# Sliding-window attention and token mixing on one core: permuted channels, weights staged in the mixing buffers, two batches of natural q and k, held stores and a new order

## The chip, the cores and the metric

The kernel runs on one core of one Trainium2 chip. The metric is the device time of one execution in microseconds (us). Three runs of the kernel before gave 143.59, 143.82 and 145.14 us, a median of 143.82 us.

The core has a matrix engine (TensorE, PE in the profile, with its weight loads as PEld), a vector engine (DVE), an activation engine (ACT), a general engine (POOL) and a queue engine (SP). Each runs its own instructions strictly in order. In this kernel POOL does almost nothing but issue the loads that change 32-bit inputs into 16-bit tiles, SP issues weight loads and stores, and ACT and DVE share the work of moving results out of PSUM, the memory that PE writes.

## The reference

Attention with a causal window of 128 tokens and a bias that falls with distance, for 8 batches of 8 heads, 576 tokens and 64 values a head; then a token-mixing layer over the 512 joined channels:

```python
scores = scale * np.matmul(q, k.transpose(0, 1, 3, 2))
mask = (rel >= 0) & (rel < window)
scores = np.where(mask, scores + bias[None], -1000000000.0)
attn = np.exp(scores - np.max(scores, axis=-1, keepdims=True))
attn = attn / (np.sum(attn, axis=-1, keepdims=True) + 1e-09)
x = np.matmul(attn, v)          # then heads joined: (8, 576, 512)
wq = x @ w_q
wk = x @ w_k                    # both 512 -> 64
W_tok = scale * np.einsum('bsd,btd->bst', wq, wk)
mixed = np.einsum('bst,btd->bsd', W_tok, x)
out = np.maximum(mixed, 0.0) @ w_out
```

## The kernel before, in words

**Attention.** The 576 tokens of a batch are four tiles of 128 and a tail of 64. POOL loads q, k and v with a cast to 16 bits, one DMA of 128 tokens x 8 heads x 64 values at a time (`Lq`, `Lk`, line 364; `Lv`, line 381; the q and k tails of two batches in `Lt`, line 371). In HBM such a tile is 1024 runs of 256 bytes. Three tiles of batch 0 are instead loaded in 32 bits by SP and ACT (`LF`, line 401) into buffers that later hold output. PE transposes q and k (`TF`, `TJ`, `TQ`, `TT`, line 235) and ACT or DVE copies them to `qkT` (`EF`, `EJ`, `ETQ`, `ETT`, lines 239 and 241). For each batch there are eight units of scores (`QK`, four key tiles times two groups of four heads): 64-row matmuls into a pair of PSUM banks, one exponential of 128 x 1024 on ACT (`EXP`, line 588) into one of the `pt` tiles, and one multiplication by the exponentiated bias and mask on DVE (`MUL`, line 595). `PV` multiplies with v, which carries a column of ones, so the sums come along. `RC` (line 649) takes reciprocals, and `X` (line 635, DVE) writes the normalised 128 x 512 tile of x in 16 bits: 32 full tiles and 8 tails of 64 rows.

**Mixing.** It is done once for each pair of batches: x is transposed (`XT`, `XTT`, copied by `EXT`, `EXTT`), then come the projections `WK`, `WQ`, `WT` with their copies `EWK`, `EWQ`, `EWT`; `G` is wk transposed times x, 64 x 512 for each batch, copied by `EG`; `MX` is the mixed tile in transposed form, to which `RM` and `RMT` (lines 771 and 773) apply the maximum with zero and write the 16-bit tile `rm`; `OUT` is four accumulating matmuls of 512 columns with `w_out`; `EO` copies the result to one of 12 32-bit output buffers (`osb`), and SP stores it (`DO`, lines 833 and 836).

**Weights.** `wz` is a memset on DVE that holds the weight loads back until DVE has come to it. `Lw` (line 441) loads `w_q` and `w_k`, in runs of 256 bytes, `Lwo` (line 449) `w_out` in four blocks of 128 rows of 2 KB. All go through SP into output buffers (`osb`). `CWQ` and `CW` copy them to 16-bit tiles, `CWQ` on ACT, `CW` on ACT and DVE. Every projection needs `CWQ`; every `OUT` needs the four `CW`.

**Order.** Nothing is scheduled automatically. A text lists every step with its engine and its PSUM bank, and each engine runs its steps in that order; waits come from data and from buffers being reused. For example `QK2.1.0:P3` is batch 2, key tile 1, head group 0, on PE, into bank pair 3; the letters A, D, G and S stand for ACT, DVE, POOL and SP. `WM` steps are matmuls on zeros whose result nobody reads. Every DMA also waits on its queue for the DMA eight places ahead of it on the same kind of queue (POOL's, or SP's and ACT's together) to land. Natural q and k tiles are kept for four batches, so a load of batch b waits for the transposes of batch b - 4; `pt` has five slots of two tiles, so an exponential waits for the `PV` steps five key tiles earlier.

Of the kernel before, what the change touches and what calls it, by code (L numbers as in the profile page):

```python
# [8 lines left out]
FP32 = mybir.dt.float32  # L9
# [5 lines left out]
P = 128  # L15
# [10 lines left out]
NNAT = 4  # L26
NV = 4
NPT = 5
# [5 lines left out]
OSB = 12  # L34
WIDE = ()

WARM = (13, 8, 2, 1, 2, 1, 4, 1, 9, 2, 6, 2, 9, 7, 1, 2, 2)

ORDER = """
warm:D LF0.0.1.1:A iota:G LF0.1.0.0:S WM.0:P01 ident:G LF0.0.1.0:A LF0.0.0.0:S wmc:D ones:D  # L40
LF0.0.0.1:S mask:G LF0.1.0.1:S Lk0.1:G bias:A Lq0.2:G idh:D TF0.1.0:P00 WM.1:P01 Lk0.2:G
EF0.1.0:D zeros:D Lk0.3:G TF0.0.0:P00 WM.2:P10 EF0.0.0:A TF0.0.1:P01 WM.3:P20 Lt0:G EF0.0.1:A
QK0.0.0:P1 TF0.1.1:P00 EXP0.0.0:A WM.4:P20 EF0.1.1:D TJ0.1.1:P01 QK0.0.1:P2 WM.5:P30 MUL0.0.0:D
Lq0.3:G EXP0.0.1:A TJ0.2.0:P00 WM.6:P30 EJ0.1.1:D Lk1.1:G EJ0.2.0:D TJ0.2.1:P10 biasl:D
QK0.1.0:P0 WM.7:P30 Lq1.1:G TJ0.3.1:P11 QK0.1.1:P2 WM.8:P31 Lq1.0:G EXP0.1.1:A MUL0.0.1:D
# [10 lines left out]
MUL1.2.1:D ETQ2.3:A PV1.1:P3 Lk2.0:G MUL1.3.1:D XT0.1:P21 RC1.0:D PV1.2:P1 RC1.1:D Lv1.4:G
pads:D EXT0.1:A wz:D X1.1:D Lwo.1:S Lv0.4:G Lw:S ETQ2.2:A X1.0:D PV1.3:P3 Lt1:G RC1.2:D Lwo.3:S
XT1.0:P00 RC1.3:D X1.2:D Lwo.0:S QK2.2.0:P2 Lwo.2:S EXT1.0:A X1.3:D TQ2.1:P01 Lq3.0:G ETQ2.1:D
XT1.1:P10 EXP2.2.0:A TQ2.0:P11 Lk3.0:G EXT1.1:A PV1.4:P0 ETQ2.0:D Lq3.1:G QK2.1.1:P3 RC1.4:D
QK2.0.0:P1 X1.4:D CWQ:A PV0.4:P2 Lk3.1:G EXP2.1.1:A WK0:P00 RC0.4:D X0.4:D Lq3.3:G EXP2.0.0:A  # L60
QK2.1.0:P3 EWK0:D QK2.0.1:P2 Lq3.2:G EXP2.1.0:A XTT0:P01 WQ0:P10 EXTT0:D Lv2.1:G EXP2.0.1:A
MUL2.1.0:D WT0:P11 Lk3.2:G MUL2.1.1:D TT2:P00 EWT0:A EWQ0:A CW.1:D G0:P01 ETT2:A ETT3:D CW.2:D
CW.3:A QK2.3.0:P1 EG0:D EXP2.3.0:A CW.0:D Lv2.3:G MX0.1:P0 MX0.0:P2 RM1.1:D MX0.3:P3 RM0.1:A
MX0.2:P1 Lv2.0:G RM1.3:A RM0.3:D TQ3.0:P00 RM1.0:A Lk3.3:G QK2.2.1:P3 ETQ3.0:D RM1.2:A TQ3.1:P01
EXP2.2.1:A RM0.2:D Lv2.2:G OUT1.0:P00 ETQ3.1:D RM0.0:A Lv3.0:G QK2.3.1:P1 MUL2.2.0:D QK3.0.0:P3
EXP2.3.1:A QK3.0.1:P2 MUL2.3.0:D Lk4.2:G OUT1.3:P01 MUL2.0.1:D EXP3.0.1:A OUT1.1:P10 Lk4.1:G
MUL2.3.1:D EXP3.0.0:A MUL2.2.1:D OUT0.1:P11 Lt2:G MUL2.0.0:D EO1.3:A TQ3.2:P20 EO1.0:A
MUL3.0.0:D PV2.1:P3 EO0.1:A ETQ3.2:D Lq4.2:G PV2.0:P0 DO1.0:S TQ3.3:P21 EO1.1:A RC2.1:D
OUT0.3:P11 X2.1:D Lv3.1:G ETQ3.3:A RC2.0:D PV2.3:P3 X2.0:D Lq4.1:G EO0.3:A QK3.1.0:P2 RC2.3:D
QK3.2.0:P0 X2.3:D EXP3.1.0:A Lv3.2:G PV2.2:P1 MUL3.0.1:D OUT1.2:P30 EXP3.2.0:A Lv3.3:G  # L70
MUL3.1.0:D XT2.0:P31 RC2.2:D Lv3.4:G EO1.2:A MUL3.2.0:D QK3.1.1:P2 QK3.3.0:P0 EXP3.1.1:A Lk4.3:G
X2.2:D OUT0.0:P30 EXT2.0:D Lq4.3:G EXP3.3.0:A QK3.3.1:P1 QK3.2.1:P2 EO0.0:D TT4:P31 Lq4.0:G
EXP3.2.1:A MUL3.1.1:D MX0.4:P0 OUT0.2:P30 MUL3.3.0:D RMT0:A Lk4.0:G PV3.0:P2 MUL3.2.1:D
EXP3.3.1:A TQ4.2:P00 Lv2.4:G ETT4:D TQ4.1:P01 ETT5:A RC3.0:D MUL3.3.1:D PV3.1:P1 Lq5.0:G EO0.2:A
OUT1.4:P31 X3.0:D ETQ4.2:A DO0.2:S Lq5.2:G RC3.1:D PV3.3:P2 DO0.0:S X3.1:D ETQ4.1:A DO0.1:S
XT2.1:P30 Lk5.0:G RC3.3:D DO0.3:S X3.3:D PV3.2:P1 EXT2.1:A Lk5.2:G QK4.1.1:P0 RC3.2:D PV3.4:P2
X3.2:D EXP4.1.1:A XT3.0:P30 Lq5.1:G RC3.4:D X3.4:D XT3.1:P10 TQ4.0:P11 Lk5.1:G EXT3.1:A EXT3.0:D
TQ4.3:P00 PV2.4:P2 Lq5.3:G ETQ4.0:D ETQ4.3:A WK2:P30 RC2.4:D Lk5.3:G X2.4:D QK4.0.1:P1 EWK2:A
MUL4.1.1:D QK4.2.0:P0 Lv4.0:G XTT2:P20 EXP4.0.1:A WQ2:P21 EXTT2:D Lv4.1:G EXP4.2.0:A WT2:P20
EWQ2:D QK4.3.1:P1 EWT2:A QK4.1.0:P0 MUL4.0.1:D EXP4.3.1:A G2:P30 Lv4.2:G EO1.4:D EXP4.1.0:A  # L80
DO1.4:S QK4.0.0:P2 EG2:D TQ5.2:P10 Lq6.2:G EXP4.0.0:A DO1.3:S MUL4.1.0:D MX2.0:P0 DO1.1:S
QK4.2.1:P3 RM2.0:D Lk6.2:G DO1.2:S EXP4.2.1:A MX2.2:P2 TQ5.0:P11 RM3.0:D Lv4.3:G RM3.2:A
ETQ5.2:D MX2.3:P3 MX2.1:P0 RM2.2:A Lq6.3:G RM2.1:D TQ5.1:P10 RM2.3:A TQ5.3:P20 RM3.1:D ETQ5.1:A
Lq6.1:G OUT2.1:P21 ETQ5.0:D RM3.3:A Lk6.1:G ETQ5.3:D QK4.3.0:P0 QK5.0.0:P1 EXP4.3.0:A QK5.0.1:P3
MUL4.0.0:D Lk6.0:G OUT2.0:P20 MUL4.2.0:D EXP5.0.1:A Lv5.1:G OUT3.1:P00 MUL4.2.1:D EO2.1:A
MUL5.0.1:D PV4.1:P3 EO2.0:A Lv4.4:G OUT2.3:P01 RC4.1:D EXP5.0.0:A MUL4.3.0:D PV4.2:P2 X4.1:D
EO2.3:A QK5.2.1:P1 RC4.2:D PV4.0:P3 X4.2:D EXP5.2.1:A OUT3.0:P01 Lv5.0:G RC4.0:D X4.0:D EO3.1:A
QK5.1.1:P2 QK5.1.0:P1 EO3.0:D EXP5.1.1:A QK5.2.0:P3 Lq6.0:G XT4.0:P00 MUL4.3.1:D OUT3.2:P01
EXP5.2.0:A EXT4.0:D Lk6.3:G MUL5.0.0:D QK5.3.0:P2 EO3.2:A Lv5.2:G PV4.3:P3 MUL5.2.1:D EXP5.1.0:A
TQ6.2:P00 Lk7.0:G RC4.3:D OUT3.3:P01 MUL5.1.1:D EXP5.3.0:A X4.3:D Lv5.3:G TQ6.1:P10 ETQ6.2:A  # L90
MUL5.2.0:D MX2.4:P2 QK5.3.1:P3 Lq7.0:G ETQ6.1:D OUT2.2:P11 EXP5.3.1:A MUL5.1.0:D Lv5.4:G
# [67 lines left out]
def kernel(  # L159
# [53 lines left out]
    def natv(b, j, n):  # L213
        return nat_s[(b // 2) % 2][j][n][:, b % 2]
# [95 lines left out]
    def mk_ones(o):  # L310
        for i in range(2):
            nc.vector.memset(vt_s[i][4][64:128], 0.0)
            for t in vt_s[i]:
                nc.vector.memset(t[:, :, :, D:D + 1], 1.0)
# [596 lines left out]
```

## Time and profile before

| What | Value |
|---|---|
| Median of three runs | 143.82 us |
| The profiled execution | 145.0 us |
| Its span, first to last instruction | 143.1 us |
| Outside the span | 1.9 us |
| Granted TensorE clock | 1.00 throughout |
| Busy: PE, DVE, ACT, POOL | 129.3, 117.5, 118.7, 95.3 us |
| HBM read, written | 29.62 MB, 9.44 MB |

Busy time by stage, from the windows of the profile, in us:

| Stage (us from the start) | length | PE | DVE | ACT | POOL |
|---|---|---|---|---|---|
| 0 to 36 | 36.0 | 30.59 | 27.60 | 27.73 | 35.16 |
| 36 to 48 | 12.0 | 8.52 | 7.83 | 8.95 | 8.94 |
| 48 to 124 | 76.0 | 75.41 | 73.10 | 74.01 | 51.15 |
| 124 to 143.1 | 19.1 | 14.75 | 9.00 | 7.99 | 0.00 |

Busy shares are averages over stages that have different limits. POOL's busy time is the issue of loads. A matmul's busy time includes its way through the array, so PE can look busier than it is. A wait is put down to whatever came last; a line number can be that of a helper that many steps share, so the operands tell which step is meant.

### The profile page before, as it was taken

How to read it: one execution, taken by the hardware profiler on the slowest of the kernel's cores; microseconds unless marked ns; L12 is line 12 of the kernel's file. 1: busy time of each engine (PE TensorE's matmuls, PEld its weight loads, DVE VectorE, ACT ScalarE, POOL GpSimd, SP SyncE). 2: the span in 40 equal slices, each digit the busy share in tenths (PEclk: the TensorE clock that was granted, in tenths of full speed). 3: DMA queues.
4: the chain of work that ended last, by engine and by line, in shares of the span. 5: the costliest groups of instructions: out<-in, count | busy, mean ns of one | idle time of the engine just before them, and what ended most of it. 6: DMA issues, size and time to landing. Idle time of an engine off the chain costs nothing.

```text
span 143.1 us, 4562 instructions
## 1 busy us (share of the span) xinstructions
PE 129.3 (90%) x1888; PEld 86.8 (61%) x1888; DVE 117.5 (82%) x253; ACT 118.7 (83%) x166; POOL 95.3 (67%) x118
## 2 busy tenths in 40 slices
PE   7979898589496999999998999999999999999980
PEld 4737776378263557678855466787665557863430
DVE  5478499988557999999879999999999999939720
ACT  4956967979398999999899999999999999867140
POOL 7999999999839999899949759998570000000000
PEclk9999999999999999999999999999999999999999
DMA  4999999999999999999999999999999941504494
GB/s 101 240 155 154 156 155 156 155 154 167 262 172 157 154 155 182 161 151 211 252 164 181 241 206 157 155 184 248 163 235 283 215 161 73 220 5 136 125 390 161
DMA packets 119333, 25.60 MB, mean 179 GB/s; under 512 B 114192, under 2 KB 114192, under 8 KB 119312
## 3 DMA queue, kind: packets, MB, share of 16 engines
q0 software_dynamic: 109264, 13.77, 151.9%
q1 hardware_dynamic: 8992, 11.28, 23.9%
q10 hardware_dynamic: 1056, 0.26, 0.8%
q8 instruction: 15, 0.25, 0.6%
q14 instruction: 6, 0.05, 0.1%
HBM read 29.62 MB, written 9.44 MB: 273 GB/s over the span
## 4 chain that ended last, share of the span: by engine, by line
PE 56%; POOL 15%; DMA 9%; DVE 7%; ACT 7%; issue 2%; SPq 0%; POOLq 0%; ACTq 0%
PE pair L232 46%; PE pair L235 11%; POOL nat L364 10%; DMA osb<-in_moe_w_k_dram 5%; DMA nat<-in_q_dram 5%; ACT pt L588 4%; POOL vt L381 3%; DVE rm L773 2%; DVE qkT L241 1%; POOL natt L371 1%; DVE osb L241 1%; DVE pt L595 1%; ACT wqT L239 1%; DVE x L635 1%; DVE wqT L241 0%
## 5 line engine op out<-in xcount | busy, mean ns | idle before, releaser
L588 ACT ACTIVATE pt<-pair 128x1024 f16<-128x1024 f32 x64 | 62.6, 1033 | 5.6 <-PE pair L232 5.1
L381 POOL DMA_DIRECT2D vt<-in_v_dram x40 | 34.7, 900 | 4.3 <-PE pair L232 2.1
L595 DVE TENSOR_TENSOR pt<-pt,bias 128x1024 f16<-128x1024 f16 x48 | 31.4, 680 | 2.9 <-ACT pt L588 2.8
L364 POOL DMA_DIRECT2D nat<-in_k_dram x31 | 28.8, 937 | 5.5 <-DMA natt<-in_k_dram 2.7
L232 PE MATMUL pair<-wout_sb,rm 128*128 128x512 f16 x128 | 31.1, 380 | 0.0
L364 POOL DMA_DIRECT2D nat<-in_q_dram x30 | 28.1, 947 | 0.7 <-PE pair L232 0.6
L232 PE MATMUL pair<-vt,pt 128*128 128x65 f16 x576 | 24.0, 193 | 1.1 <-DVE x L635 0.5
L232 PEld LDWEIGHTS <-pt 128*128 128x128 f16 x576 | 21.2, 97 | 6.3 <-issue 2.9
L232 PE MATMUL pair<-qkT 64*128 64x256 f16 (+2 forms) x320 | 21.6, 250 | 1.0 <-ACT pt L588 0.7
L635 DVE TENSOR_TENSOR x<-pair,inv 128x512 f16<-128x512 f32 x32 | 21.8, 687 | 0.8
L235 PE MATMUL pair<-identh,nat 128*128 128x128 f16 x244 | 18.6, 219 | 1.6 <-DMA nat<-in_k_dram 0.8
L239 ACT COPY osb<-pair 128x512 f32<-128x512 f32 x25 | 14.5, 609 | 5.0 <-PE pair L232 5.0
L232 PEld LDWEIGHTS <-rm 128*128 128x128 f16 x128 | 11.2, 98 | 11.7 <-issue 0.6
L235 PEld LDWEIGHTS <-nat 128*128 128x128 f16 x244 | 14.5, 97 | 5.5 <-DMA nat<-in_k_dram 1.9
L241 DVE COPY qkT<-pair 128x1024 f16<-128x1024 f16 (+1 forms) x26 | 15.2, 592 | 2.2 <-PE pair L235 1.1
L232 PEld LDWEIGHTS <-qkT 64*128 64x128 f16 x320 | 11.1, 94 | 8.5 <-issue 5.4
L239 ACT COPY qkT<-pair 128x1024 f16<-128x1024 f16 (+1 forms) x15 | 13.5, 916 | 0.9 <-PE pair L235 0.9
L232 PE MATMUL pair<-warm 128*128 128x256 f16 x72 | 12.0, 299 | 1.6 <-DVE warm L282 1.1
L239 ACT COPY xT<-pair 128x1024 f16<-128x1024 f16 x12 | 12.1, 1027 | 1.1 <-PE pair L235 0.8
L595 DVE TENSOR_TENSOR pt<-pt,biasl 128x1024 f16<-128x1024 f16 x16 | 10.8, 681 | 0.4 <-ACT pt L588 0.2
L771 ACT ACTIVATE rm<-pair 128x512 f16<-128x512 f32 x18 | 9.7, 618 | 0.6 <-PE pair L232 0.6
L235 PE MATMUL pair<-identh,x 128*128 128x128 f16 x128 | 9.6, 219 | 0.5 <-ACT pt L588 0.5
(69 smaller groups left out, 135.9 us busy)
## 6 DMA issues: line engine op xcount, KB each, us to landing
out_dram<-osb SPq DMA_DIRECT2D x32, 256.0 KB, 4.4
vt<-in_v_dram POOLq DMA_DIRECT2D x32, 128.0 KB, 6.8
nat<-in_k_dram POOLq DMA_DIRECT2D x31, 128.0 KB, 6.3
nat<-in_q_dram POOLq DMA_DIRECT2D x30, 128.0 KB, 6.5
osb<-in_moe_w_out_dram SPq DMA_DIRECT2D x4, 256.0 KB, 6.9
out_dram<-osb SPq DMA_DIRECT2D x8, 128.0 KB, 4.3
osb<-in_q_dram SPq DMA_DIRECT2D x4, 128.0 KB, 3.6
natt<-in_q_dram POOLq DMA_DIRECT2D x4, 128.0 KB, 6.1
```

The source lines that it names most:

```text
L232: hold(nc.tensor.matmul(*a, **k))
L235: hold(nc.tensor.transpose(*a))
L239: hold(nc.scalar.copy(out_ap, in_ap))
L241: hold(nc.vector.tensor_copy(out=out_ap, in_=in_ap))
L364: return lambda: nc.gpsimd.dma_start(out=natv(b, j, n), in_=(q, k)[j][b, :, P * n:P * n + P, :].transpose([1, 0, 2]))
L371: nc.gpsimd.dma_start(out=natt_s[pr % 2][:, j].rearrange("p e h d -> p (e h) d"), in_=(q, k)[j][2 * pr:2 * pr + 2, :, 512:576, :].rearrang ...
L381: return lambda: nc.gpsimd.dma_start(out=vtv(b, t)[:n, :, 0:D], in_=v[b, :, P * t:P * t + n, :].transpose([1, 0, 2]))
L588: nc.scalar.activation(out=pt[:, 0:1024], in_=two(s.bank).rearrange("p e c -> p (e c)"), func=AF.Exp, scale=SCALE)
L595: ENG2[o.eng].tensor_tensor(out=pt[:, 0:1024], in0=pt[:, 0:1024], in1=bt, op=ALU.mult)
L635: nc.vector.tensor_tensor(out=x[r].rearrange("p (g h d) -> p g h d", g=2, h=4), in0=sums(p)[r, :, :, 0:64], in1=box["inv"][r].unsqueeze(3) ...
L771: hold(nc.scalar.activation(out=out_ap, in_=in_ap, func=AF.Relu, scale=WSCALE))
L773: hold(nc.vector.tensor_scalar(out=out_ap, in0=in_ap, scalar1=0.0, scalar2=WSCALE, op0=ALU.max, op1=ALU.mult))
```

## The change

- **Channels of x.** `X` writes column `128*c + p` of its tile with channel `4*p + c`, so its four parts of 128 columns hold every fourth channel. The weights' rows are taken in the same way: `w_q` and `w_k` are each read as 128 runs of 1 KB, `w_out` in two loads of 128 runs of 4 KB.
- **Staging.** The weights lie, until they are cast, in the two `rm` buffers instead of the output buffers; the first `RM` steps wait for the casts. `wz` is two memsets. `CWQ` also turns the order of its columns.
- **Buffers.** Natural q and k for two batches instead of four, `pt` with eight slots instead of five, 15 output buffers instead of 12.
- **Held stores.** From batch 3 on, a step `GT b.g` on SP makes the next store wait for the first `QK` of that key tile; it issues nothing by itself.
- **Last output.** Tile 3 of batch 7 is made in two halves of 256 columns, each with its own copy and store.
- **Order.** A new text. `pads` moves to the start. 107 matmuls on zeros instead of 72. Between ACT and DVE some copies change places.
- Groups of batches become a table; all groups are still pairs, and the code for single batches is not used.

The core of the diff:

```diff
-NNAT = 4
+NNAT = 2
-NPT = 5
+NPT = 8
-OSB = 12
+OSB = 15
+GATES = 3
+GROUPS = ((0, 1), (2, 3), (4, 5), (6, 7))
+SPLIT = ((7, 3),)
...
-    nat_s = [[[cpool.tile([P, 2, H, D], F16, name=f"nat{i}{j}{n}") for n in range(4)]
-              for j in range(2)] for i in range(2)]
+    nat_s = [[[cpool.tile([P, H, D], F16, name=f"nat{i}{j}{n}") for n in range(4)]
+              for j in range(2)] for i in range(NNAT)]
...
+            wst = [t.rearrange("p d e t -> p (d e t)").bitcast(FP32) for t in rm_s]
+            def mk_wz(o):
+                for t in wst:
+                    nc.vector.memset(t[:, 0:1], 0.0)
...
-                    nc.sync.dma_start(out=dst[:, :, 64 * j:64 * j + 64],
-                                      in_=w.rearrange("(c p) j -> p c j", p=P))
+                    nc.sync.dma_start(out=wst[0][:, 256 * j:256 * j + 256],
+                                      in_=w.rearrange("(p c) j -> p (c j)", p=P))
...
-                      lambda o: cp(o.eng, wqk_sb.rearrange("p c j -> p (c j)"), wide32("qk")))
+                      lambda o: cp(o.eng, wqk_sb.rearrange("p c (m j) -> p m c j", m=2),
+                                   wst[0][:, 0:512].rearrange("p (m c j) -> p m c j", m=2, c=4)))
...
-                    out=wide32(c), in_=moe_w_out[P * c:P * c + P, :]))
+                    out=wst[1][:, 1024 * u:1024 * u + 1024],
+                    in_=moe_w_out.rearrange("(p c) n -> p (c n)", p=P)[:, 1024 * u:1024 * u + 1024]))
...
+        if u == 0 and b >= GATES:
+            add("GT", b, g, w, {"SP": (0.02, 0.02)}, [s], lambda o: gates.append(s))
...
-                out=x[r].rearrange("p (g h d) -> p g h d", g=2, h=4),
-                in0=sums(p)[r, :, :, 0:64],
-                in1=box["inv"][r].unsqueeze(3).broadcast_to([n, 2, 4, 64]),
+                out=x[r].rearrange("p (c g h t) -> p g h t c", c=4, g=2, h=4),
+                in0=sums(p)[r, :, :, 0:64].rearrange("p g h (t c) -> p g h t c", c=4),
+                in1=box["inv"][r].unsqueeze(3).unsqueeze(4).broadcast_to([n, 2, 4, 16, 4]),
                 op=ALU.mult)
...
+            old = [osd.get((x, st)) for x in prev for st in range(4)] if prev else [*wto, wts]
...
+    def gated(i):
+        while gates:
+            tc.add_manual_dep(
+                i.ins, gates.pop().insts[-1].name,
+                mybir.DependencyInfo(mybir.DependencyClass.Sync, mybir.DependencyReason.DATA),
+                reason="stores behind loads")
...
+        if (b, st) in SPLIT:
+            add_out_cols(b, st, want, 0, 256, st)
+            add_out_cols(b, st, want, 256, 512, st + 5)
```

The order where the weights arrive, each engine's own steps in sequence, from the text before and after:

```
before
ACT  EXT0.0 ETQ2.3 EXT0.1 ETQ2.2 EXT1.0 EXP2.2.0 EXT1.1 CWQ EXP2.1.1 EXP2.0.0 EXP2.1.0 EXP2.0.1 EWT0 EWQ0 ETT2 CW.3 EXP2.3.0 RM0.1
PE   PV1.4 QK2.1.1 QK2.0.0 PV0.4 WK0 QK2.1.0 QK2.0.1 XTT0 WQ0 WT0 TT2 G0 QK2.3.0 MX0.1 MX0.0 MX0.3 MX0.2 TQ3.0
DVE  X1.4 RC0.4 X0.4 EWK0 EXTT0 MUL2.1.0 MUL2.1.1 CW.1 ETT3 CW.2 EG0 CW.0 RM1.1
after
ACT  ETQ2.2 EXT0.0 ETQ2.3 EXT0.1 EXT1.1 EXP2.2.0 EXT1.0 EXP2.0.0 CWQ EXP2.1.0 EXP2.1.1 CW.3 EXP2.2.1 EXP2.0.1 EWQ0 EG0 ETQ3.1 RM0.1
PE   PV0.4 QK2.0.0 PV1.4 QK2.2.1 QK2.1.0 QK2.1.1 XTT0 WK0 WT0 WQ0 QK2.0.1 TT2 G0 TQ3.1 MX0.1 MX0.2 MX0.3 MX0.0 TQ3.0
DVE  X0.4 RC1.4 X1.4 EXTT0 EWK0 EWT0 CW.0 CW.2 MUL2.2.0 CW.1 ETT2 ETT3 MUL2.1.1 RM1.1
```

And the end of it:

```
before
PE   XT7.1 OUT5.2 MX4.4 XTT6 WK6 WT6 WQ6 G6 OUT5.4 MX6.4 MX6.3 MX6.2 MX6.1 MX6.0 OUT7.4 OUT6.0 OUT7.0 OUT7.1 OUT7.2 OUT6.1 OUT6.2 OUT6.3 OUT7.3
last EO6.3 and EO7.3 on ACT, then DO7.3
after
PE   XT7.1 OUT5.2 MX4.4 XTT6 WK6 WT6 WQ6 G6 OUT5.4 MX6.4 MX6.1 MX6.2 MX6.0 MX6.3 OUT7.4 OUT6.1 OUT6.3 OUT6.2 OUT6.0 OUT7.0 OUT7.2 OUT7.1 OUT7.8 OUT7.3
last EO7.3, then EO7.8 on DVE, then DO7.3, DO7.8 (OUT7.8 and DO7.8 are the second half of tile 3)
```

More of the change, by code (lines that the diff above doesn't have):

```diff
@@ L56 @@
[L56 to L91, printed above, removed]
@@ L323, in mk_pads @@
     def mk_pads(o):
+        for t in xone_s:
+            nc.vector.memset(t[64:128], 0.0)
         for t in wkt_s:
```

388 lines of the change are left out of this document (224 added, 164 removed).

## The prediction

> **What bounds the kernel now.** I read the slices of the page first, to see which engine is full where.
>
> ```profile
> DVE  5478499988557999999879999999999999939720
> ACT  4956967979398999999899999999999999867140
> POOL 7999999999839999899949759998570000000000
> ```
>
> A slice is 3.58 us. POOL, which issues the loads, is full up to about 36 us while DVE and ACT have gaps. All three sag in slices 10 to 12 (36 to 46 us). Then DVE and ACT are full to about 124 us, and the end is thin on both. The windows of 4 us put numbers on that; the columns are length, then busy time of PE, PEld, DVE, ACT, POOL, each with its count, then clock, DMA share and GB/s.
>
> ```profile
> 36.00:40.00 4.00, 1.89 (x47) 1.43 (x44) 1.79 (x4) 1.57 (x3) 2.79 (x4) 1.00 1.64 262
> ...
> 44.00:48.00 4.00, 2.63 (x32) 1.24 (x30) 3.28 (x7) 3.43 (x7) 3.88 (x6) 1.00 2.39 153
> 48.00:52.00 4.00, 4.00 (x40) 2.08 (x41) 4.00 (x7) 3.91 (x7) 4.00 (x5) 1.00 2.41 155
> ...
> 132.00:136.00 4.00, 4.00 (x20) 1.83 (x19) 2.96 (x5) 0.83 (x2) 0.00 (x0) 1.00 0.52 136
> ```
>
> So there are four stages: loads to 36 us; a hole, 36 to 48 us, in which DVE is idle 12.0 - 7.83 = 4.2 us and ACT 3.1 us; DVE and ACT together from 48 to 124 us (idle 2.9 and 2.0 us of 76); and a last stage of PE and stores. The chain that ended last, in order of time (start, length, what), names the cause of the hole:
>
> ```profile
> 31.51 0.37 SPq L441
> 31.88 0.04 issue
> 31.92 6.73 DMA osb<-in_moe_w_k_dram
> 38.65 0.02 issue
> 38.67 0.63 ACT wqk_sb L239
> 39.30 0.04 issue
> 39.34 1.66 PE pair L232 x40
> ```
>
> The mixing weights are the wait. The timeline shows who stands behind them; the last bracket is the engine's idle time before and its end:
>
> ```profile
> 35.22 1.02 ACT L239 COPY xT<-pair 128x1024 f16<-128x1024 f16 x1
> 38.67 0.62 ACT L239 CAST wqk_sb<-osb 128x512 f16<-128x512 f32 x1 [2.43 <-DMA osb<-in_moe_w_k_dram]
> ...
> 39.34 1.09 PE L232 MATMUL pair<-wqk_sb,xT 128*128 128x64 f16 x32 [2.07 <-ACT wqk_sb L239]
> ```
>
> **Weights: when they land.** `wz` is at 31.42 us. In the new order one `X` more stands ahead of it and `RC1.0`, `RC1.1` and `pads` fewer, and the v tile that this `X` needs is load 25 instead of 26; I leave it there (1 us either way). By the packets in windows of 1 us, nothing of `w_q` and `w_k` moves before 33.8 us; then their 1024 packets go at 513 and 373 per us, beside POOL's loads, which fall from 1213 packets per us to 455. `w_out`, behind them on the same queue, moves from 36.3 to 40.1 us at 109 to 112 packets of 2 KB per us, 225 GB/s. After: 256 packets of 1 KB. At 225 GB/s, 0.26 MB is 1.2 us, so 33.8 to 35.0; `w_k` landed some 1.7 us behind its last packets, so 36.7 us instead of 38.65. Bounds: 34.8 (the shortest staged load, 2.9 us) and 38.65 (nothing gained). `w_out` is now 1.05 MB there, because one of its four blocks was loaded at 2.9 us before: 4.7 us at 225 GB/s, 35.0 to 39.7, landed at about 40.4; bounds 39.5 (the 4 KB runs take a larger share) and 42.5 (9.5 us from issue, as POOL's loads of this time took).
>
> **Weights: what that frees.** Until 36.24 us ACT does the same seven steps from `EXT0.0` on, and one exponential more, 1.03: it reaches `CWQ` at 37.3 without a wait. `XTT0` needs the last `X` of batches 0 and 1, which ends at 38.3 and depends on v loads in the same places (32 and 33) of POOL's list, so this does not move. From there PE has XTT0 0.40, WK0 1.0, WT0 0.5, WQ0 1.0, QK2.0.1 0.25, TT2 0.55, G0 1.3: 5.0 us, done at 43.3 (before 44.5). ACT goes CWQ to 37.9, two exponentials to 40.0, then `CW.3`, which now waits for the second half of `w_out` until 40.4; 0.63 for it, two exponentials 2.06, EWQ0 0.58, EG0 0.58 make 44.25, and `MX0` can start at 44.3. Before it started at 46.12. Both orders have by then 22 exponentials and 18 multiplications behind them; the new one has no other arrears. Gain: **-1.8 us**.
>
> **The hole's other loads.** `TT2` and, new there, `TQ3.1` stand ahead of `MX0` on PE. Their last load starts at about 33.5 and landed 9.5 us later in this stretch: 43.0. Covered, with 0.3 us to spare.
>
> **X with its columns spread.** 40 instructions on DVE. The reading side is unchanged in length; each write now lands 256 bytes from the one before. Nothing in the trace writes 512 values so. The nearest row is a memset of 16 values at steps of 132 bytes, beside one of 32 contiguous values and one of a single value (mean ns of one at the end):
>
> ```profile
> L635 DVE TENSOR_TENSOR x<-pair,inv 128x512 f16<-128x512 f32 x32 | 21.8, 687 | 0.8
> ...
> L314 DVE MEMSET vt<- 128x16 f16 x10 | 0.7, 72 | 0.2
> ...
> L321 DVE MEMSET pt<- 128x32 uint32 x10 | 0.4, 85 | 0.0
> ...
> L436 DVE MEMSET osb<- 128x1 f32 x1 | 0.1, 59 | 0.0
> ```
>
> Spread: (72 - 59)/15 = 0.87 ns a value; contiguous: (85 - 59)/31 = 0.84. I take no cost. The upper bound is a doubled rate: DVE copies 256 values of PSUM in 424 ns and 512 in 685, 1.02 ns a value, so +0.52 us each and 20.9 us over 40. A gain is excluded: as many values are read from PSUM, one by one, as before.
>
> The Trainium skill, SBUF — State Buffer, section Door 1, speaks against this edit: successive accesses in one 16-byte line run at full rate, and each access that goes to a new line pays. By it `X` gets dearer by an amount that the page does not give. The Trainium skill, VectorE: DVE Perf Modes, section Mode 1×, says the opposite for this kind of instruction: its plain mode takes any stride and any PSUM operand at one result a cycle; the memsets agree with that one, on 16 values only.
>
> **DVE and ACT, 48 to 124 us.** Copies that change engine: ACT gives away three `ETQ` (1.03 each), two `EWK`, two `EWQ` and smaller ones and takes two `EXT`, five `RM`, one `RMT`, one `EG`: -0.7 us by their mean durations; DVE +0.5. Nothing on the sum of two full engines. Their idle time there, 2.4 us in the mean, can at best vanish; eight `pt` slots and a new order can also add to it. I take a third back, **-0.8 us** (0 to -2.4; the other way, below).
>
> **Two batches of q and k.** 109 loads at 0.88 us stay. A load of batch b now waits on POOL for the transposes of b - 2, and everything behind it on POOL, the v loads, waits too. First place that can bite: `Lk6.3` behind `TQ4.3`, about 70 us; before, POOL stood still there as well, 1.79 us for a v buffer. v of batch 4 is needed some 10 us later against 6.7 us to land. Nothing, with one such stall, up to 2.7 us (the longest of the trace), as bound.
>
> **Held stores.** SP has only stores behind the gates. The buffers they hold: 15, the first three used by the 32-bit loads; the first copy that reuses a gated one is `EO3.2`, on the buffer of `EO1.3`, whose store goes after `QK4.1.0`, well ahead. Nothing; uncovered, one landing, 4.4 us. Loads beside stores landed in 8.1 us against 6.2, but hardly anybody waits for a load after 48 us, so no gain either.
>
> **Small things.** 35 more zero matmuls of about 0.13 us, in PE's waits before 36 us; 6 more memsets of 85 ns; `pads` at the start: under the load stage, nothing (uncovered at most 4.5 us of PE).
>
> **The end.** The same steps stand from the last `X` to the last `OUT`. The halves don't overlap: PE makes the second half first, DVE copies it second. So after the last matmul come two copies of 0.42 us instead of one of 0.58, then a 128 KB store (4.3 us against 4.4 for 256 KB, medians): **+0.2 us** (-0.3 to +0.5).
>
> **Sum.** -1.8 - 0.8 + 0.2 = -2.4 us. The profiled execution took 145.0 us (span 143.1 and 1.9 around it), so 142.6 for that one; it lies 1.2 above the median of 143.82, from which I subtract: **141.4 us**.
>
> **Rivals.** *The wait moves to `w_out`.* `CW.3` now stands on ACT ahead of two exponentials, `EWQ0` and `EG0`. If its half lands at 42.5, `MX0` starts at 46.4: the 1.8 becomes +0.3, and the time 143.5. For it: POOL's loads took 9.5 us in this stretch. Against: the 225 GB/s. The same follows, at 142.4, if run length does not matter and `w_k` lands at 38.65 as before.
> *The spread write costs.* On DVE, line 635. 30 of the 40 lie in batches 2 to 7, where DVE is full: from 2.4/30 = 80 ns each the gain is gone; at a doubled rate +15.7 us on those alone, 157, up to 162 with all.
> *POOL stalls.* Each wait for a transpose that pushes the v loads into DVE's full stage costs up to 2.7 us; two of them: 146.8. Against: 51 of 76 us busy there.
> *More than the sum.* The full stage loses all its idle time and `MX0` comes at its earliest, 43.9: -2.2 - 2.4 + 0.2, 139.4; gaps before 36 us closed as well, 138.
>
> **Numbers.** A change of this kernel shows from about 1%, 1.4 us. Forecast, a gain of 1 to 5 us: 0.58. More than that: 0.08. Wait moved or nothing gained, 142.4 to 145.2: 0.17. Stalls, 145.3 to 147: 0.07. Spread write: 0.10. So faster 0.66, same 0.17, slower 0.17. Range 138.4 to 145.6: it leaves out the largest gains, the spread write and half of the stalls.
>
> **What would show it.** `CWQ` with no idle time for a DMA and at about 37.3; `MX0` near 44.3; `X` at 687 ns; DVE and ACT still full until about 121.5; the last DVE copies back to back. `X` at 0.77 us or more, or ACT idle before `CW.3` for over 2 us, would make the prediction wrong.

## The result, and the profile after

| | median, us | runs | lowest to highest |
|---|---|---|---|
| before | 143.70 | 4 | 143.27 to 145.14 |
| after | 212.92 | 4 | 212.16 to 214.30 |

The ratio is 1.485 (95% interval 1.478 to 1.492): the changed kernel is 69 us slower. Some executions of a kernel here took over 1.5% longer than its fastest, and the ratios leave them out. The profiled execution of the changed kernel took 213.46 us, its span is 211.5 us, the mean granted TensorE clock 0.852.

The slices of the page after (one digit for each of 40 equal slices, now 5.29 us long) stand against those of before:

```profile
DVE  5764999997699999989999999999899999995651
ACT  6667871334649955713389775452597943151431
POOL 8999999619991920000999789600000000000000
...
PEclk9999979755589999955699999787699999557998
```

Before, DVE and ACT were full together. Now DVE alone is full from slice 5 to slice 36 (21 to 190 us), with one dip at 48 to 60 us, and ACT stands at 3 to 7 for most of that time: one engine holds up all the others. The groups by line and shape say which instruction does it (busy us, mean ns of one, then idle time before it):

```profile
L657 DVE TENSOR_TENSOR x<-pair,inv 128x512 f16<-128x512 f32 x32 | 77.0, 2463 | 0.8
...
L657 DVE TENSOR_TENSOR xtl<-pair,inv 64x512 f16<-64x512 f32 x8 | 19.7, 2458 | 0.3
```

These are the 40 `X` instructions, 687 and 689 ns before. 32 x 1.776 + 8 x 1.769 us = 71.0 us more on DVE; the span grew by 68.4 us. No other group of DVE or ACT came near that: `MUL` went from 680 to 711 ns, `EXP` stayed at 1.03 us. The chain that ended last, of which `X` was no named part before, now begins with it:

```profile
DVE x L657 30%; PE pair L248 27%; DVE xtl L657 9%; DVE pt L617 8%; PE pair L251 6%; DVE qkT L257 3%; DVE inv L671 3%; ACT pt L610 2%; DVE osb L257 1%; ACT qkT L255 1%; ACT rm L804 1%; DVE rm L806 0%; DVE xT L257 0%; ACT wkt L255 0%; ACT gs 
```

The waits (total us, times, longest) show how it spreads. POOL's loads wait for transposes on PE, ACT waits for PE's scores and transposes, and PE waits for `X`:

```profile
POOL nat L378 <- PE pair L251: 36.9, 3, 25.4
ACT pt L610 <- PE pair L248: 28.4, 22, 4.8
...
PE pair L248 <- DVE x L657: 18.7, 14, 1.7
```

In the windows the clock that PE is granted sinks to 0.50 and comes back, where it was 1.00 throughout before. The columns are as in the prediction; the third number from the end is the clock:

```profile
48.00:60.00 12.00, 8.69 (x108) 6.23 (x108) 8.81 (x13) 5.91 (x7) 12.00 (x15) 0.50 2.07 132
60.00:72.00 12.00, 11.51 (x129) 6.36 (x126) 11.56 (x21) 11.09 (x16) 6.98 (x9) 1.00 1.43 111
```

Matmuls take longer at the low clock: a transpose of x, 219 ns before, takes 311 ns at 49 us. What sets the clock is not shown; from 72 to 84 us PE is busy for less, 7.55 us, at 1.00. The longer matmuls account for little of the loss: DVE's busy time grew by 66.1 us (117.5 to 183.6), its idle time by 2.3 us (25.6 to 27.9). DVE stays the full engine.

### The profile page after: what moved, and what is told of

It is laid out like the page before. It is cut to its first block, busy times and chain, and to the rows that moved or that the text cites. A ratio compares the mean times of both kernels' runs of the same rounds, so it can differ in the third digit from the quotient of the medians.

```text
span 211.5 us, 4647 instructions
## 1 busy us (share of the span) xinstructions
PE 157.5 (75%) x1927; PEld 106.4 (50%) x1927; DVE 183.6 (87%) x261; ACT 120.6 (57%) x166; POOL 95.4 (45%) x118
## 4 chain that ended last, share of the span: by engine, by line
DVE 53%; PE 32%; issue 8%; ACT 4%; DVEq 0%
DVE x L657 30%; PE pair L248 27%; DVE xtl L657 9%; DVE pt L617 8%; PE pair L251 6%; DVE qkT L257 3%; DVE inv L671 3%; ACT pt L610 2%; DVE osb L257 1%; ACT qkT L255 1%; ACT rm L804 1%; DVE rm L806 0%; DVE xT L257 0%; ACT wkt L255 0%; ACT gs L255 0%
## 5 line engine op out<-in xcount | busy, mean ns | idle before, releaser
L657 DVE TENSOR_TENSOR x<-pair,inv 128x512 f16<-128x512 f32 x32 | 77.0, 2463 | 0.8
L248 PE MATMUL pair<-vt,pt 128*128 128x65 f16 x576 | 28.5, 209 | 19.2 <-DVE x L657 9.7
L248 PEld LDWEIGHTS <-pt 128*128 128x128 f16 x576 | 26.2, 108 | 25.8 <-issue 21.4
L248 PE MATMUL pair<-wout_sb,rm 128*128 128x512 f16 (+1 forms) x132 | 31.9, 381 | 0.1
L257 DVE COPY qkT<-pair 128x1024 f16<-128x1024 f16 (+1 forms) x30 | 18.3, 628 | 5.9 <-PE pair L251 4.8
L657 DVE TENSOR_TENSOR xtl<-pair,inv 64x512 f16<-64x512 f32 x8 | 19.7, 2458 | 0.3
L251 PE MATMUL pair<-identh,x 128*128 128x128 f16 x128 | 14.1, 273 | 7.6 <-DVE x L657 4.1
L248 PE MATMUL pair<-warm 128*128 128x256 f16 x107 | 18.3, 303 | 1.1 <-DVE warm L298 1.1
L251 PEld LDWEIGHTS <-x 128*128 128x128 f16 x128 | 10.7, 124 | 8.9 <-DVE x L657 4.9
L255 ACT COPY qkT<-pair 128x1024 f16<-128x1024 f16 (+1 forms) x11 | 9.8, 896 | 6.6 <-PE pair L251 5.2
```

What stands on the lines that cost most here:

```text
L248: hold(nc.tensor.matmul(*a, **k))
L251: hold(nc.tensor.transpose(*a))
L255: hold(nc.scalar.copy(out_ap, in_ap))
L257: hold(nc.vector.tensor_copy(out=out_ap, in_=in_ap))
L657: nc.vector.tensor_tensor(out=x[r].rearrange("p (c g h t) -> p g h t c", c=4, g=2, h=4), in0=sums(p)[r, :, :, 0:64].rearrange("p g h (t c) ...
```

## The experiments

Times of experiments are compared with runs of the kernel before on the same chip. Ratios have their 95% interval.

### Is it X alone, and is the rest worth its forecast?

**The permutation alone.** The kernel before, with only the spread write and the matching rows of the weights:

```diff
-                out=x[r].rearrange("p (g h d) -> p g h d", g=2, h=4),
-                in0=sums(p)[r, :, :, 0:64],
-                in1=box["inv"][r].unsqueeze(3).broadcast_to([n, 2, 4, 64]),
+                out=x[r].rearrange("p (c g h t) -> p g h t c", c=4, g=2, h=4),
+                in0=sums(p)[r, :, :, 0:64].rearrange("p g h (t c) -> p g h t c", c=4),
+                in1=box["inv"][r].unsqueeze(3).unsqueeze(4).broadcast_to([n, 2, 4, 16, 4]),
...
-                                      in_=w.rearrange("(c p) j -> p c j", p=P))
+                                      in_=w.rearrange("(p c) j -> p c j", p=P))
```

> The kernel before, with one part of the change: X writes its columns spread and the rows of the weights are taken in the order that this needs, their runs as long as before. Theory A: X takes 2463 ns here too, 40 x 1.77 us = 71 us more on DVE; the time is 205 to 215 us. Rival C, that X is slow only in the changed kernel (its other buffers, or the traffic beside it): X at 687 ns and 143.7 us, or something clearly under 200 us.

Measured: 215.82 us, 0.8 us over theory A's range; a second execution took 220.81 us. `X` takes 2444 ns, its tails 2430 ns:

```profile
L635 DVE TENSOR_TENSOR x<-pair,inv 128x512 f16<-128x512 f32 x32 | 77.5, 2444 | 1.1
```

The one edit, without new buffers, order or stores, brings the whole loss. Rival C falls.

**Everything but the permutation.** The changed kernel with the same lines of `X` and of the weight loads put back (runs of 256 bytes and 2 KB, still staged in the `rm` buffers).

> Everything of the change but the permutation: X is written in natural column order and the weight loads keep runs of 256 B and 2 KB, still staged in the mixing buffers. Theory A, that X alone is the cause: X is back at 687 ns and the time is near the 141.4 us of the prediction, 140 to 144. Rival B, that the rest of the change costs too (stalls of POOL, held stores, the end): above 145.2, up to 147, and the waits name it. In between, 142.4 to 145.2, the weights stage gave nothing back: MX0 then starts at 45.5 us or later instead of 44.3.

Measured: 144.16 us in the profiled execution, just outside theory A's range; three others took 146.6 to 147.4 us. One execution cannot tell A from B, so the kernel was run again beside the one before:

> Everything of the change but the permutation, a second time, to be set beside the kernel before on one chip. If the prediction's other terms held, 2.4 us less than before (141.2 or so); by the first look, where MX0 came 0.2 us earlier than before and the end 0.9, between -1 and +1 us.

Measured: ratio 1.0096 (1.0046 to 1.0146), about 1.4 us slower than before. `X` is at 687 ns again. So `X` explains the 70 us, and the rest of the change is no gain either. The forecast of -2.4 us counted on long runs of the weights, which this kernel lacks; the next one has them. The second part of the study, below, goes after that.

**The permutation on PE.** `X` writes in natural order; the transposes take every fourth column of x as weights, and so does `MX` from its left operand. The weights keep their long runs.

```diff
-                    tp(dst[:, c, n, :], x_s[b % NX][2 * i + n][:, P * c:P * c + P], identh)
+                    tp(dst[:, c, n, :], x_s[b % NX][2 * i + n].rearrange("p (k c) -> p c k", c=4)[:, c, :], identh)
...
-                    lhs = gs_s[sl][half(e), P * d:P * d + P]
+                    lhs = gs_s[sl][half(e), :].rearrange("p (k c) -> p c k", c=4)[:, d, :]
```

> The whole change with its 1 and 4 KB runs of the weights, but X is written in natural order and PE does the permutation: the transposes of x, and the mixing matmuls of their left operand, read every fourth column as their weights (208 weight loads with steps of 8 bytes). Theory A1, that only a writing engine pays for steps: weight loads stay near 124 ns, X at 687 ns, and the time is that of the kernel with the permutation taken out, less what longer runs bring (up to 1.8 us). Rival, that any engine pays about 3.5 ns for a value at such a step: 128 x 3.5 ns = 0.44 us for each weight load, 92 us on the weight side of PE, and a time above 180 us.

Measured: ratio 1.0083 (1.0036 to 1.0130), about 1.2 us slower than before where -2.4 us was forecast for all but `X`. `X` takes 687 ns. A weight load of x at 8-byte steps takes 114 ns against 97 ns in natural order, the transposes stay at 219 ns. The weight loads of this kernel, then those of the kernel before:

```profile
L251 PEld LDWEIGHTS <-x 128*128 128x128 f16 x128 | 7.8, 114 | 0.0
```

```profile
L235 PEld LDWEIGHTS <-x 128*128 128x128 f16 x128 | 7.6, 97 | 1.7 <-issue 0.9
```

Theory A1 holds: the same permutation costs 1.8 us a tile as a write on DVE, and next to nothing as a read on PE.

### What in the write costs 1.8 us?

**Ten patterns.** In the kernel before, the 32 whole `X` were written in ten orders, each on a line of its own, for example steps of 16 bytes and of 8 bytes with an innermost loop of 64, and runs of four values:

```diff
+                tt(out=x[r].rearrange("p (d g h) -> p g h d", g=2, h=4), in0=src, in1=i4, op=M)
...
+                tt(out=x[r].rearrange("p (g d h) -> p g h d", g=2, h=4), in0=src, in1=i4, op=M)
...
+                tt(out=x[r].rearrange("p (t g h c) -> p g h t c", g=2, h=4, c=4), in0=s5, in1=i5, op=M)
```

> The kernel before, in which the 32 X of whole tiles are written in ten patterns, each on a line of its own, so that x has its columns in another order and the output is not that of the reference. Four memsets of 512 f16 values stand before the first load: contiguous, in steps of 256 bytes (innermost loop of 4), in steps of 64 bytes (32 values only), in steps of 8 bytes (innermost loop of 128). Theory W (a write that leaves its 16-byte line pays, about 3.5 ns): steps of 32, 128 and 256 bytes with an innermost loop of 4 all take 2460 ns; steps of 16 bytes with an innermost loop of 64 take 2460 too; runs of 4 values, each 64 bytes on, take a quarter of the excess, 1130; steps of 8 bytes half of it, 1570; steps of 4 bytes a quarter, 1130. Theory L (an innermost loop of only 4 costs a restart of 13.9 ns): all patterns with an innermost loop of 4, the runs of 4 too, take 2460 ns, whatever their step, and those with an innermost loop of 64 stay at 690. Theory D (only steps as long as 256 bytes pay): 2460 ns for 256 bytes alone, less for 128, 690 for 32. X in two halves should take about 2 x 370 ns; runs of 16 values with PSUM read at steps of 16 bytes, two halves, the same by W and L, and clearly more if the reading side pays. By W the spread memset takes some 1.8 us more than the contiguous one.

The groups of DVE by shape, in this kernel (L649 natural, L651 steps of 32 bytes, L655 of 256 as in the change, L657 of 16, L661 of 8, L663 of 4, L659 runs of four values 64 bytes apart, L669 halves with PSUM read in steps; L326 the spread memset):

```profile
L651 DVE TENSOR_TENSOR x<-pair,inv 128x512 f16<-128x512 f32 x4 | 9.3, 2334 | 0.1
...
L655 DVE TENSOR_TENSOR x<-pair,inv 128x512 f16<-128x512 f32 x3 | 7.3, 2432 | 0.2
L657 DVE TENSOR_TENSOR x<-pair,inv 128x512 f16<-128x512 f32 x3 | 7.3, 2430 | 0.1
...
L661 DVE TENSOR_TENSOR x<-pair,inv 128x512 f16<-128x512 f32 x3 | 3.9, 1300 | 0.1
L649 DVE TENSOR_TENSOR x<-pair,inv 128x512 f16<-128x512 f32 x4 | 2.7, 684 | 0.1
...
L669 DVE TENSOR_TENSOR x<-pair,inv 128x256 f16<-128x256 f32 x6 | 2.3, 418 | 0.1
L663 DVE TENSOR_TENSOR x<-pair,inv 128x512 f16<-128x512 f32 x3 | 2.2, 740 | 0.0
L659 DVE TENSOR_TENSOR x<-pair,inv 128x512 f16<-128x512 f32 x3 | 2.1, 687 | 0.1
...
L326 DVE MEMSET x<- 128x512 f16 x1 | 0.5, 485 | 1.9 <-issue 1.9
```

Theory L is out: an innermost loop of 64 with 16-byte steps costs 2430 ns, and one of four values in a run costs nothing. Theory D is out: 32 bytes cost nearly as much as 256 (2334 against 2432 ns). Reading PSUM in steps costs nothing (418 ns against 420 for natural halves). Theory W is right in direction, but its sizes do not fit: it gave 1130 ns for the runs of four (687 measured) and for 4-byte steps (740), 1570 ns for 8-byte steps (1300), and 1.8 us more for the spread memset (nothing). What fits the ten writes of `X` within 5% is a floor and not a surcharge: 162 ns + 4.44 ns for each visit to a 16-byte stretch (162 ns are the fixed part of DVE's PSUM copies, 685 - 512 x 1.02, as the prediction had it; 4.44 is (2436 - 162)/512, from the steps of 128 bytes). With 512 visits that is 2435 ns, with 256 it is 1299, with 128 it is 730; an `X` takes the longer of that and its reading time of 687 ns. The run of four is a little under it. And the memset of 512 values at 256-byte steps takes 485 ns, what a contiguous one takes.

**Other runs, other operations.** Runs of two, four and eight values, and single operations on idle buffers before the weights arrive, in order and spread: multiplication, copy, copy to f32, on ACT and on POOL.

> The kernel before, whole X in four patterns (natural; runs of 2 values, 4 and 8, each run in another 16-byte line than the last), so that x has other columns and the output is not the reference's; and a row of single operations of 512 values each on idle buffers ahead of the weights. Theory V, from the ten patterns: an X takes the longer of its reading time, 687 ns, and 162 ns + 4.44 ns for each visit to a 16-byte line. Runs of 2 make 256 visits, 1300 ns; runs of 4 and 8 make 128 and 64, 687 ns. If it holds for any write, the spread forms of a multiplication from SBUF, of a DVE copy, of a copy to f32, of an ACT copy and of a POOL copy all take 2400 ns or more, and reading spread is as fast as reading in order. Rival P, that it comes from reading PSUM and writing spread at once: the spread forms from SBUF stay at the time of their contiguous forms, as the memset did. Rival E, that it is DVE's alone: ACT's spread copy takes what its contiguous one takes.

L671 is `X` in runs of two; L333 to L335 are the multiplication from SBUF in order, written spread, and read spread:

```profile
L671 DVE TENSOR_TENSOR x<-pair,inv 128x512 f16<-128x512 f32 x8 | 5.5, 689 | 0.2
...
L334 DVE TENSOR_TENSOR x<-x 128x512 f16<-128x512 f16 x1 | 2.4, 2432 | 0.0
...
L335 DVE TENSOR_TENSOR x<-x 128x512 f16<-128x512 f16 x1 | 1.2, 1218 | 0.0
...
L333 DVE TENSOR_TENSOR x<-x 128x512 f16<-128x512 f16 x1 | 0.4, 424 | 0.0
```

The multiplication from SBUF takes 2432 ns written spread and 424 ns in order, so PSUM has no part in it and rival P falls. Reading SBUF spread is not free, against theory V's expectation: with both operands read at 256-byte steps and the result in order it takes 1218 ns, and a DVE copy read so takes 593 ns against 295. Rival E falls with ACT and POOL. In the groups of this kernel L342 and L344 are the spread copies of ACT and POOL (618 and 609 ns in order), L337 is DVE's (half as dear, 295 ns in order), L340 the copy to f32 in steps of 512 bytes (418 ns in order):

```profile
L342 ACT COPY x<-x 128x512 f16<-128x512 f16 x1 | 2.5, 2473 | 0.0
L344 POOL COPY x<-x 128x512 f16<-128x512 f16 x1 | 2.5, 2461 | 0.1
...
L337 DVE COPY x<-x 128x512 f16<-128x512 f16 x1 | 1.3, 1305 | 0.0
...
L340 DVE CAST rm<-x 128x512 f32<-128x512 f16 x1 | 0.7, 691 | 0.0
```

But an `X` in runs of two values, each in another 16-byte stretch, took 689 ns where theory V had 1300, and f32 values, one to a stretch, 691 ns. Both write whole 4-byte words. So visits as such do not cost 4.44 ns; those that leave half a word unwritten do. That is theory H.

**Half words.** It was put to a test that keeps the number of runs, their length and their distance, and moves them by one value:

```diff
+        nc.vector.tensor_tensor(out=r8[:, 0:256, 0:2], in0=z2, in1=z2, op=ALU.mult)
+        nc.vector.tensor_tensor(out=r8[:, 0:256, 1:3], in0=z2, in1=z2, op=ALU.mult)
+        nc.vector.tensor_tensor(out=r8[:, 0:170, 0:3], in0=z3, in1=z3, op=ALU.mult)
+        nc.vector.tensor_tensor(out=r8[:, 0:128, 0:4], in0=z4, in1=z4, op=ALU.mult)
+        nc.vector.tensor_tensor(out=r8[:, 0:128, 1:5], in0=z4, in1=z4, op=ALU.mult)
```

> The kernel before, with a row of single operations on idle buffers ahead of the weights; sources are contiguous f16 in SBUF, targets are groups of 1 to 4 f16 values, each group 16 bytes after the last. Theory H (a write that leaves half of a 4-byte word unwritten costs about 4.5 ns, writes to one 16-byte stretch that follow each other counted once; whole words cost nothing more): single values, even or odd place, 2430 ns; aligned pairs 420 to 690; pairs shifted by one value, the same number of bytes in the same runs, 256 x 4.44 + 162 = 1300; triples 170 visits, 920; aligned fours 420 to 690; shifted fours 128 visits, 730 or a little more. Rival R (only the length of a run counts): shifted pairs and fours take what aligned ones take. The memset of 512 single values at 16-byte steps: 485 if a memset never pays, 2430 if the one with 256-byte steps was spared by its long step. A DVE copy of single values from f32: 1305 as from f16, or 2430 as for the multiplication and ACT. ACT: aligned pairs 620, shifted pairs 1300 by H and 620 by R.

The groups of this kernel; L337 to L341 are the five lines of the diff, L344 and L345 pairs and shifted pairs on ACT:

```profile
L345 ACT COPY rm<-x 128x512 f16<-128x512 f16 x1 | 1.3, 1335 | 0.0
L338 DVE TENSOR_TENSOR rm<-x 128x512 f16<-128x512 f16 x1 | 1.3, 1294 | 0.0
L339 DVE TENSOR_TENSOR rm<-x 128x510 f16<-128x510 f16 x1 | 0.9, 910 | 0.0
L341 DVE TENSOR_TENSOR rm<-x 128x512 f16<-128x512 f16 x1 | 0.7, 728 | 0.0
L344 ACT COPY rm<-x 128x512 f16<-128x512 f16 x1 | 0.6, 645 | 16.2 <-DVE rm L343 16.2
L337 DVE TENSOR_TENSOR rm<-x 128x512 f16<-128x512 f16 x1 | 0.6, 612 | 0.0
...
L340 DVE TENSOR_TENSOR rm<-x 128x512 f16<-128x512 f16 x1 | 0.4, 427 | 0.0
```

Shifting pairs by one value doubles their time on DVE (612 to 1294 ns, 1300 expected) and on ACT (645 to 1335); triples 910 (920 expected), shifted fours 728 (730 expected) against 427. Single values: 2425 ns in even places, 2646 in odd ones. Rival R falls. The triples start on a whole word and pay all the same, so it is not the place of the start that counts. Whole words spread are not quite free either: the aligned pairs' 612 ns stand against 424 ns in order, and the f32 copy's 691 against 418; under an `X` of 687 ns this does not show. The spread memset again took 485 ns, so its spread is free at 16-byte steps too; a DVE copy of single values from f32 took 1367 ns.

### Where did the forecast gain of the rest go?

**Before, on the same chip.** Two profiles of the kernel before, to judge how far a single one can be trusted.

> The kernel before, unchanged, for its stages on the same chip as the next two: a span of 141.4 to 143.1 us, MX0 at 45 to 46.2 us, the last matmul at 137.5 to 139.

Measured: a span of 143.8 us, MX0 at 45.6, the last matmuls from 132.3 to 139.4 us; the span and the end are later than expected. The execution took 145.56 us, 1.8 us above the median of the 19 runs of the same kernel beside it (143.77 us). Its second transposes of 32-bit data started at 5.94 us, against 4.98 us in the first profile: the eight matmuls on zeros ahead of them took 417 ns each, against 273, though the loads landed no later (median 3.4 us from issue, against 3.6). By MX0 this was made up (45.6 against 46.1), and yet the last matmul ended 0.5 us later. The gain or loss of the rest is therefore read from medians, and from the traces only which wait stands where.

**Which wait stands at the weights.** In the trace of the permutation on PE, ACT's instructions at the place of the former hole read (last bracket: idle time before, and what ended it):

```profile
38.28 0.64 ACT L255 CAST wqk_sb<-rm 128x512 f16<-128x512 f32 x1
38.79 1.97 ACT L610 ACTIVATE pt<-pair 128x1024 f16<-128x1024 f32 x2
42.49 0.62 ACT L255 CAST wout_sb<-rm 128x512 f16<-128x512 f32 x1 [1.73 <-DMA rm<-in_moe_w_out_dram]
```

`CWQ` has lost its wait of 2.4 us, and `CW.3` has gained one of 1.73 us, with `EG0`, and so MX0, behind it. MX0 starts at 46.0 us, against 46.1 before. Long runs are only a part of why `CWQ` no longer waits: in the new order ACT reaches it at about 38.4 us instead of 36.2, and with short runs the wait is 0 to 0.9 us in five traces. In the two traces without the permutation the wait for `w_out` was 1.36 and 0.74 us. So the copies were moved in that kernel:

```diff
-WQ0:P10 CW.3:A EWT0:D EXP2.2.1:A
+WQ0:P10 EWT0:D EXP2.2.1:A
...
-Lq3.2:G CW.2:D EXP2.0.1:A
+Lq3.2:G EXP2.0.1:A
...
-MUL2.1.1:D ETQ3.1:A MX0.1:P0
+MUL2.1.1:D ETQ3.1:A CW.2:D CW.3:A MX0.1:P0
```

> The same, with the two copies CW.2 and CW.3 of the second half of w_out moved behind EG0 in the order of DVE and ACT. Theory O (the wait for w_out has taken the place of the wait for w_k): without the 1.36 us wait and the 0.62 us of the copy ahead of EG0, EG0 starts at 43.5 instead of 45.2 and MX0 at 44.2 instead of 45.9; of these 1.7 us the end gets 0.8 to 1.7. Rival: MX0 comes earlier, but the same copies, now behind it, hold up OUT1.0 and the exponentials behind it, and the end is within 0.5 us of the kernel without the move.

Measured: MX0 at 44.5 us against 45.9, the last run of `OUT` matmuls at 131.2 us against 131.6; ratio to before 1.0079 (1.0036 to 1.0122), against 1.0096 without the move. The wait was there and is gone, but of 1.4 us at MX0 0.4 us reach the end in these two traces: the rival's outcome in size. The ratios agree, with intervals that overlap. The following stage gives the rest back in several small waits (`DVE qkT` for PE 1.4 us in all, POOL for its own earlier loads), none of which stands out.

**Long runs alone.** The kernel before with its order and buffers, the weights in runs of 1 and 2 KB, the permutation on PE:

```diff
-                    nc.sync.dma_start(out=dst[:, :, 64 * j:64 * j + 64],
-                                      in_=w.rearrange("(c p) j -> p c j", p=P))
+                    nc.sync.dma_start(out=wide32("qk")[:, 256 * j:256 * j + 256],
+                                      in_=w.rearrange("(p c) j -> p (c j)", p=P))
```

> The kernel before, its order and buffers kept, with the weight part alone: w_q and w_k come in runs of 1 KB into the same buffer, rows of w_out in the matching order, and PE reads every fourth column of x and of the mixing operand as weights; X writes in natural order. If the run length sets when w_k lands, as the prediction had it, w_k lands 1.5 to 1.9 us earlier than 38.2 to 38.7, the wait of 2.4 us ahead of CWQ goes to 0.5 to 0.9, MX0 comes 1.4 us earlier, and the time falls by 0.4 (what the kernel with the moved copies passed on to the end) to 1.5 us. Rival: the load engines are shared with POOL's loads and the landing does not move; then 0 +- 0.5 us.

Measured: ratio 1.0155 (1.0102 to 1.0209). `w_k` took 5.7 us from issue to landing (6.6 and 6.7 before), the wait ahead of `CWQ` fell to 1.3 us of DMA, MX0 stayed at 45.8 us. The kernel is slower than before by more than either theory allowed, and why is open. With the new order the same runs landed in 4.1 to 4.6 us, the short ones in 5.2 to 6.1. Long runs help by about 1.3 us at the landing; no gain in time came from it alone.

**Held stores.** The kernel without the permutation, and with no `GT` steps:

```diff
-GATES = 3
+GATES = 99
```

> The kernel without the permutation (runs of 256 B and 2 KB, staged in the mixing buffers, new order), in which stores are no longer held back until the QK matmuls of later tiles. If holding costs nothing, as the prediction had it, the same time as with it, 0.96% above before, +- 0.5%. If it is the hold that makes this kernel 1.3 us slower than before, it comes back to the time of before.

Measured: ratio 1.0176 (1.0135 to 1.0217), against 1.0096 with held stores. Holding is not what makes the rest slow. That it saves time is not shown: the two ratios come from different chips, and on the chip of this run the kernel of the next trial, stores held, stood at 1.0153.

**Zero matmuls.** Two groups of them stand before `PV` and transposes that ACT waits for at 30 to 35 us. They were cut alone:

```diff
-WARM = (13, 5, 1, 2, 4, 1, 8, 5, 5, 5, 3, 2, 2, 12, 2, 4, 1, 7, 2, 2, 5, 1, 1, 2, 7, 5)
+WARM = (13, 5, 1, 2, 4, 1, 8, 5, 5, 5, 3, 2, 2, 12, 2, 4, 1, 7, 2, 2, 5, 1, 1, 2, 1, 1)
```

> The kernel without the permutation (256 B and 2 KB runs), with one edit: the last two groups of zero matmuls, 7 and 5 long, are 1 long. If they cost what they stand for in front of PV and the transposes that ACT waits for at 30 to 35 us (0.8 + 0.5 us of PE, of which the trace shows 0.2 to 0.3 us as waits of others), the time falls by 0.5 to 1.3 us, to about that of before. If they lie under other work, as the prediction had it: no change, 0.96% above before +- 0.5%.

Measured: ratio 1.0153 (1.0093 to 1.0213), from three executions; no gain. ACT's wait of 1.51 us became one of 1.18 us for DVE's reciprocals: another cause stood behind the first. That they cost anything, against the forecast, is not shown.

**All together.** Permutation on PE, moved copies, the two short groups:

> The whole change with the permutation on PE, the copies CW.2 and CW.3 behind EG0, and the last two groups of zero matmuls cut from 7 and 5 to 1 each. w_k lands at 37.1, ACT's two waits for PE at 30 to 35 us (1.5 and 0.8 us) shrink by up to 0.7 each, CWQ starts at 37.2 to 37.9 without a wait, MX0 at 42.5 to 43.5. By the earlier trial little of this reaches the end, a third: 0.8 us less than the kernel with the permutation on PE alone, or 143.8 against 144.6; if all reached it, 142.

Measured: median 143.40 us, ratio 1.0008 (0.9972 to 1.0043). ACT waits for no DMA between 36 and 48 us any more. Each edit alone had brought 0.2% or less; with all of them the 1% is gone. The trace does not show where: its `CWQ` starts at 39.0 us and its MX0 at 44.7, later than the 37.2 to 37.9 and 42.5 to 43.5 expected, and its execution, at 144.37 us, was the slowest of the ten. That each had only uncovered the other wait, `w_k` or `w_out`, fits the traces (0.44 us for `w_k` was left where only the copies were moved), but it was not shown separately. Cutting 30 more zero matmuls (67 are left of the changed kernel's 107, so 40 fewer and not 41),

> The version with the permutation on PE, the moved copies and the cut, with every group of zero matmuls from the twelfth on 1 long (41 fewer). If zero matmuls stand in the way of real ones: up to 1 us less than 143.4. If they are needed to keep PE's clock granted: the clock before 40 us falls below 1.00 and the time rises. Else 143.4 +- 0.5.

gave a ratio of 1.0045 (1.0017 to 1.0073): no gain. In the profiled execution the clock stayed at 1.00 up to 52 us; two of the eleven others had a mean clock of 0.97. The best version of the change is thus as fast as the kernel before, and none is shown faster.

## Why the prediction was wrong

- **X with its columns spread**: this step failed, and it alone brings the result (215.82 us with nothing else changed). The prediction took no cost, from a memset of 16 values at 132-byte steps; measured were 1.77 us more for each `X`, 71 us in all. The analogy was wrong and not the sample too small: a memset of 512 values at 256-byte steps is as fast as a contiguous one, while every operation tried that reads something and writes single 16-bit values pays. The upper bound, a doubled rate, was an assumption with no row behind it; the duration came to 3.6 times that of before, and 162 us at the far end of the rival became 213. The rival's mechanism and place (DVE, line 635, full from batch 2 on) were right, its price too low, its chance of 0.10 far too low.
- The Trainium skill, SBUF — State Buffer, section Door 1, warned of accesses that go to a new line. The runs agree that the spread write pays and that neighbours within 16 bytes share the cost, but not that a new line pays as such: an `X` in pairs of values that fill a 4-byte word, each on a new line, takes 689 ns.
- The Trainium skill, VectorE: DVE Perf Modes, section Mode 1×, gives one result a cycle at any stride. For strides in SBUF the runs differ: 512 results took 2432 ns written spread and 1218 ns read spread, against 424.
- **Weights, when they land**: for `w_k` the size was right, 37.1 us in the trace with the permutation on PE, 36.7 forecast, partly by luck: it was issued 1.1 us later than in the kernel before (33.0 against 31.9), where the prediction had left the time as it was, and took 4.1 us. For `w_out` the step failed: 40.4 us was taken, 42.5 came, the upper bound. About 1 us of that is the later issue (34.0 us, and 8.5 from there); and the 225 GB/s of before did not carry over, and 4 KB runs landed no earlier than 2 KB ones (42.3 us).
- **What that frees**: `CWQ` without a wait was right, its time (37.3) 1.0 us early, because ACT gets two waits for PE in the new order (1.5 and 0.8 us) that the count of steps had left out. MX0 came at 46.0 us, not 44.3: the first rival, a wait that moves to `w_out`, as it was worked out (46.4).
- **The sum** let each microsecond at MX0 reach the end. One trial moved MX0 by 1.4 us and the end by 0.4.
- **DVE and ACT, -0.8 us**: not separable; together with all else but the write of `X` (the permutation on PE), +0.8%, where the forecast was -1.7%. Two traces without the permutation (spans of 142.2 and 142.7 us) even end before the two of before (143.1 and 143.8), but these two were executions 1.2 and 1.8 us above their median; the ratios decide. Which of the new order, the buffers and two batches of q and k costs that, stays open; buffers and batches were not tried alone.
- **Held stores**: forecast at nothing; a cost is not shown, nor is a saving. **Zero matmuls**: nothing, and nothing else is shown. **The end**: the two half copies stand back to back as forecast; from the last matmul's end to the span's end are 4.0 us against 4.2, so -0.2 instead of +0.2.

## What to carry to other kernels

Before an operand's layout is changed, see whether the writing instruction still fills whole 4-byte words: 16-bit results set down one by one cost 3.6 times the instruction here, and the engine that does it was the full one. Take a price only from a row that reads and writes as the new instruction does; a memset is not such a row, and where no row exists, that is a reason for a wide range. If a layout must be permuted, let the reading side do it, PE's weight loads or a PSUM operand in steps: both were free here to within some 20 ns. A DVE operation that reads SBUF in steps is no such place: the multiplication read at 256-byte steps took 1218 ns against 424.

## What the runs showed of the hardware

- 16-bit values written singly to SBUF, each in another 16-byte stretch, cost about 4.4 ns each as a multiplication on DVE (2432 ns for 512, 424 in order), and about as much as a copy on ACT (2473, 618 in order) and POOL (2461, 609). Writes that follow each other into one 16-byte stretch share one such cost (740 ns for an `X` with four to a stretch, 1300 with two), and whole 4-byte words do not pay it (612 ns for aligned pairs, 1294 for shifted ones). Why a half word costs that is not shown.
- DVE's copies pay about half of it (1305 ns from f16, 1367 from f32) and its memset nothing (485). No reason for either was found.
- TensorE's granted clock was 0.50 at 48 to 60 us of the changed kernel, with PE busy for 8.69 of these 12 us, and 1.00 in the next 12 us. What sets it is not shown.
- A DVE multiplication that reads both operands from SBUF at 256-byte steps took 1218 ns against 424, an `X` half that reads PSUM at 16-byte steps 418 against 420.
- Two profiles of the kernel before differ by 0.5 us at MX0 one way and by 0.7 us in the span the other way, and the same matmuls on zeros took 273 ns in one and 417 in the other, so that a profile of one execution can contradict the medians in a question of 1%.
